# Interleaving transposes with output matmuls, a wider accumulating DMA and a reordered start in a kernel that mixes seven taps and applies a gated two-layer map

## The chip, the cores and the metric

The kernel runs on 1 core of one Trainium2 chip. The metric is device microseconds (us) of one execution. Kernels are compared only within the same rounds.

Short names: PE is the engine of the matmuls, ACT that of activations, DVE the vector engine, POOL the GpSimd engine. A "block" is 1024 tokens; there are 32, numbered 0 to 31.

## The reference, cut to what matters

```python
# x: (8, 4096, 192); weight_gen: (8, 4096, 8 heads, 7 taps)
w = exp(weight_gen - max) / sum                      # softmax over the 7 taps
x_pad = concatenate([zeros(6 rows), x])              # a "halo" of 6 rows ahead of each batch
y[b,s,h,g] = sum_k w[b,s,h,k] * x_pad[b, s+k, h, g]  # 7 products, summed
h = y @ w_in                                         # 192 -> 2048
out = (h - tanh(h)) @ w_out                          # 2048 -> 192
```

## The kernel before

For each block POOL computes the seven products of x with the softmax weights, each 1536 elements in each of 128 partitions. From block 3 on, taps 0, 2, 4 lie in `even`, taps 1, 3, 5 in `odd`, tap 6 in `last`, and a DMA that POOL issues adds `odd` to `even`, so that PE has fewer pieces to sum:

```python
# products(n): on POOL, k = 0..6
if k == K - 2 and in_pairs:                          # after tap 5, before tap 6
    nc.gpsimd.dma_start(out=even[...][:, 0:ACC], in_=odd[...][:, 0:ACC],
                        accum_op=mybir.AluOpType.add, max_dma_last_dim=4096)
# ACC leaves out the last 512 columns, so PE sums one piece of odd itself:
groups = [even[:, i] for i in range(NPAIR)] + [last[:]]
prods_of[n] = [groups + ([odd[:, NPAIR - 1]] if c == NC - 1 else []) for c in range(NC)]
```

PE then transposes and sums the pieces in one go, with matmuls against the identity that accumulate in PSUM (the lines "pc" of the profile). 104 of them make a block's `convT`. The first layer (`gemm1`, "ph") makes 16 f tiles of 128 hidden columns; ACT takes the tanh of each (`th`) and DVE subtracts (`gt`). The second layer (`gemm2`, "obank") makes one of 8 output tiles at a time, for the block before. The pools:

```python
xpool  = tc.tile_pool(name="xpool", bufs=2)          # the x of a block
ppool  = tc.tile_pool(name="ppool", bufs=2)          # even, odd, last
psum_h = tc.tile_pool(name="psum_h", bufs=3, ...)    # shared by ph (f tiles) and pc (transposes)
...
for n in range(NTOT):
    load_wg(n + 3); load_x(n + 3)                    # cases of the first and last blocks, softmax: cut
    for p in range(J):                               # 8 steps: 2 f tiles, 1 output tile
        gemm1(n, 2 * p); gemm1(n, 2 * p + 1)
        gemm2((n - 1) * J + p)
        if p == 0: products(n + 2, behind=last_sub[0])   # POOL may start here, not sooner
        if p == 6: conv(n + 1, (0, 1)); conv(n + 1, (2,))   # the transposes
```

The softmax here doesn't subtract the row's maximum and nothing guards it: scores larger than these inputs give would overflow.

## Time and profile before

770.52 us, median of 3 runs (770.43 to 771.18). The page's busy times and instruction queues:

```profile
PE 736.7 (96%) x14784; PEld 583.1 (76%) x14784; DVE 652.9 (85%) x595; ACT 640.8 (83%) x865; POOL 695.2 (90%) x290
...
q0 software_dynamic: 10816, 31.99, 25.8%
q8 instruction: 115, 1.88, 1.0%
```

The first line is busy us, share of the span and instructions. In the queue lines the columns are packets, MB and share of 16 DMA engines; q0 carries the accumulations, q8 the instructions.

| quantity | value | from |
|---|---|---|
| span | 768.7 us | page |
| PE block without a fetch wait ("undisturbed") | 22.63 us | first transposes at 591.31, 613.94, 636.57 |
| POOL period | 22.656 us | accumulations from block 4 (98.46) to block 31 (710.17), 27 periods |
| distance, POOL's last accumulation to PE's transposes of the same block | 16.92 us | 727.09 - 710.17 |
| transposes to the end | 41.64 us | 768.73 - 727.09 |

The distance rests on these two lines of the timeline (columns as explained below):

```profile
710.17 1.20 POOL L201 DMA_DIRECT2D even<-odd  x1 [0.30 <-POOL odd L192]
...
727.09 0.88 PE L233 MATMUL pc<-ident,even 64*128 64x64 bf16 x48
```

A "fetch wait" is a wait of PE that has no releaser in the trace.

Two views are easily misread. POOL at 90% looks less loaded than PE at 96%; but POOL has nothing to do in the last 55 us, and where it works it works back to back. And in the list of waits, "issue" is a wait with no releaser in the trace, not work.

### The profile page before, as it was taken

The page shows a single profiled execution, that of the slowest core. Times are in us where ns is not written, and L with a number is a line of the kernel's source. Part 1 is how long each engine was busy: PE and PEld are TensorE (multiplying, and loading weights), DVE is VectorE, ACT ScalarE, POOL GpSimd, SP SyncE. Part 2 cuts the span into 40 slices and gives each one's busy share as a digit, 9 for nine tenths or more (in the row PEclk, how much of TensorE's full clock was granted, in tenths as well). Part 3 has the DMA queues.
Part 4 walks back from the last instruction along what each step waited for, and adds up shares of the span by engine and source line. Part 5 has one row for each costly group of instructions (what it writes and reads, how often), then busy time and mean ns, then how long its engine had stood idle before and what let it go on. Part 6 is the DMA issues. An engine that isn't in the chain of part 4 may idle for free.

```text
span 768.7 us, 32330 instructions
## 1 busy us (share of the span) xinstructions
PE 736.7 (96%) x14784; PEld 583.1 (76%) x14784; DVE 652.9 (85%) x595; ACT 640.8 (83%) x865; POOL 695.2 (90%) x290
## 2 busy tenths in 40 slices
PE   2799999999999999999999999999999999999997
PEld 2377787777777777788777777777778777787777
DVE  5987888888898888889888888888888988888883
ACT  1777878888888888888888888888888888888883
POOL 5999999999999999999999999999999999999100
PEclk9999999999999999999999999999999999999999
DMA  7823776555677555577655557765556765542412
GB/s 209 184 81 87 182 181 150 118 145 147 169 182 174 131 129 148 150 180 182 164 123 133 150 160 182 180 128 137 143 150 172 182 181 115 125 142 72 98 43 84
DMA packets 25847, 111.37 MB, mean 145 GB/s; under 512 B 4800, under 2 KB 9456, under 8 KB 21624
## 3 DMA queue, kind: packets, MB, share of 16 engines
q1 hardware_dynamic: 14688, 76.95, 29.9%
q0 software_dynamic: 10816, 31.99, 25.8%
q8 instruction: 115, 1.88, 1.0%
q10 hardware_dynamic: 208, 0.39, 0.2%
q14 instruction: 20, 0.16, 0.1%
HBM read 54.49 MB, written 25.17 MB: 104 GB/s over the span
## 4 chain that ended last, share of the span: by engine, by line
PE 93%; DVE 2%; issue 1%; POOL 1%; DMA 1%; ACT 1%; SPq 0%; POOLq 0%
PE ph L257 43%; PE obank L289 43%; PE pc L233 6%; DVE gt L269 2%; PE po L323 1%; DMA x_t<-in_x_dram 1%; POOL even L192 1%; ACT th L267 0%; ACT convT L244 0%; POOL odd L192 0%; DVE zr L151 0%; DVE zsum L145 0%; SPq L117 0%; SPq L93 0%; SPq L121 0%
## 5 line engine op out<-in xcount | busy, mean ns | idle before, releaser
L269 DVE TENSOR_TENSOR gt<-ph,th 128x1024 bf16<-128x1024 f32 x512 | 602.8, 1219 | 93.3 <-ACT th L267 92.7
L267 ACT ACTIVATE th<-ph 128x1024 f32<-128x1024 f32 x512 | 497.2, 1022 | 65.7 <-PE ph L257 64.9
L257 PE MATMUL ph<-convT,w_in 64*128 64x512 bf16 x3072 | 382.1, 378 | 7.5 <-DVE gt L269 5.0
L289 PEld LDWEIGHTS <-gt 64*128 64x128 bf16 x7936 | 345.1, 94 | 53.4 <-issue 2.5
L289 PE MATMUL obank<-w_out,gt 64*128 64x192 bf16 x7936 | 374.6, 243 | 2.9 <-issue 2.1
L192 POOL TENSOR_TENSOR even<-x_t,wsm 128x1536 bf16<-128x1536 f32 x94 | 272.8, 2903 | 3.9 <-DMA x_t<-in_x_dram 1.6
L192 POOL TENSOR_TENSOR odd<-x_t,wsm 128x1536 bf16<-128x1536 f32 x93 | 269.9, 2903 | 0.0
L257 PEld LDWEIGHTS <-w_in 64*128 64x128 bf16 x3072 | 180.1, 94 | 108.4 <-issue 11.8
L192 POOL TENSOR_TENSOR last<-x_t,wsm 128x1536 bf16<-128x1536 f32 x31 | 103.4, 3336 | 0.0
L307 ACT ACTIVATE out_sb<-obank 128x192 f32<-128x192 f32 x248 | 81.9, 330 | 10.5 <-PE obank L289 4.6
L244 ACT ACTIVATE convT<-pc 128x1024 bf16<-128x1024 f32 x64 | 48.9, 808 | 31.6 <-PE pc L233 31.5
L233 PE MATMUL pc<-ident,even 64*128 64x64 bf16 x2304 | 47.9, 192 | 2.9 <-POOL even L192 1.5
L233 PEld LDWEIGHTS <-even 64*128 64x128 bf16 x2304 | 42.7, 96 | 4.1 <-issue 2.2
L201 POOL DMA_DIRECT2D even<-odd x29 | 34.9, 1205 | 9.1 <-POOL odd L192 9.1
L163 POOL TENSOR_TENSOR wsm<-e_t,zr 128x448 f32<-128x448 f32 x30 | 41.7, 1390 | 0.0
L233 PE MATMUL pc<-ident,odd 64*128 64x64 bf16 x448 | 15.5, 198 | 13.1 <-DVE odd L192 12.8
L135 ACT ACTIVATE e_t<-wg_t 128x448 f32<-128x448 f32 x32 | 18.5, 578 | 8.2 <-DMA wg_t<-in_weight_gen_dram 8.2
L233 PE MATMUL pc<-ident,last 64*128 64x64 bf16 x768 | 23.3, 192 | 1.8 <-issue 1.7
L145 DVE TENSOR_REDUCE zsum<-e_t 128x64 f32<-128x448 f32 x32 | 19.5, 609 | 2.9 <-ACT e_t L135 2.9
L233 PEld LDWEIGHTS <-odd 64*128 64x128 bf16 x448 | 11.3, 100 | 13.6 <-DVE odd L192 12.9
L151 DVE RECIPROCAL zr<-zsum 128x64 f32<-128x64 f32 x30 | 16.6, 553 | 3.0
L233 PEld LDWEIGHTS <-last 64*128 64x128 bf16 x768 | 17.0, 96 | 2.2 <-issue 1.8
(20 smaller groups left out, 48.7 us busy)
## 6 DMA issues: line engine op xcount, KB each, us to landing
x_t<-in_x_dram SPq DMA_DIRECT2D x24, 1344.0 KB
even<-odd POOLq DMA_DIRECT2D x29, 1024.0 KB, 8.8
out_dram<-out_sb SPq DMA_DIRECT2D x31, 768.0 KB
x_t<-in_x_dram SPq DMA_DIRECT2D x8, 1176.0 KB
wg_t<-in_weight_gen_dram SPq DMA_DIRECT2D x32, 224.0 KB
x_t<-in_x_dram SPq DMA_DIRECT2D x8, 157.5 KB
w_in<-in_moe_w_in_dram POOLq DMA_DIRECT2D x6, 128.0 KB, 7.5
w_out<-in_moe_w_out_dram POOLq DMA_DIRECT2D x1, 768.0 KB, 10.8
```

The lines of the kernel that those rows point to most:

```text
L135: nc.scalar.activation(out=e_t[:].rearrange("p j h k -> p (j h k)"), in_=wg_t[:].rearrange("p j h k -> p (j h k)"), func=ACT.Exp,)
L145: nc.vector.reduce_sum(out=zsum[:], in_=e_t[:].rearrange("p j h k -> p (j h) k"), axis=AX.X)
L163: return eng.tensor_mul(wsm.rearrange("p j h k -> p (j h) k"), e_t[:].rearrange("p j h k -> p (j h) k"), zr.rearrange("p (n o) -> p n o", ...
L192: eng.tensor_mul(dst[k].rearrange("p c j h g -> p j h c g"), x_t[:, k : k + J, :].rearrange("p j (h c g) -> p j h c g", h=H, c=NC), w[:, : ...
L201: nc.gpsimd.dma_start(out=even[:].rearrange("p i c j h g -> p (i c j h g)")[:, 0:ACC], in_=odd[:].rearrange("p i c j h g -> p (i c j h g)" ...
L233: nc.tensor.matmul(pc[:, r, col : col + R], lhsT=prods[c][gi][r * R : (r + 1) * R, c, 2 * j : 2 * j + 2].rearrange("p j h g -> p (j h g)") ...
L244: nc.scalar.activation(out=convT[:, c0 : c0 + nch, :].rearrange("p c (j r t) -> p r (c j) t", r=2, t=R), in_=pc[:, :, 0 : nch * JH * R].re ...
L257: nc.tensor.matmul(ph[:, r, :], lhsT=w_in[r * R : (r + 1) * R, c, f * P : (f + 1) * P], rhs=convT[r * R : (r + 1) * R, c, :], start=(c == ...
L267: last_act[0] = nc.scalar.activation(out=th[:], in_=ph_f, func=ACT.Tanh)
L269: last_sub[0] = nc.vector.tensor_sub(gt[:], ph_f, th[:])
L289: mm = nc.tensor.matmul(po[:, 0:D], lhsT=g_of[n][f][r * R : (r + 1) * R, col : col + P], rhs=w_out[r * R : (r + 1) * R, f, :], start=(r == ...
L307: last_act[0] = nc.scalar.activation(out=out_sb[:, j, :], in_=po[:, 0:D], func=ACT.Copy)
```

## The change

The intent: alternate 50 of the transposes with output matmuls, so that PE does not run through its instructions in a burst; put four f-tile steps of the next output tile (the filler) behind the transposes, where PE waits for a PSUM buffer; let the DMA add all of the pairs, so that the last 8 transposes go; load the first x tile ahead of its halo rows, so that POOL starts sooner. The core of the diff (the helper functions it needs are cut):

```diff
-    ACC = NPAIR * J * D - J * R
...
+        if n == 0:
+            rows(0, P, HALO, HALO + J)
+            rows(16, P, 0, HALO)
+            rows(1, 16, 0, HALO)
+            no_halo()
...
-                    out=even[:].rearrange("p i c j h g -> p (i c j h g)")[:, 0:ACC],
-                    in_=odd[:].rearrange("p i c j h g -> p (i c j h g)")[:, 0:ACC],
+                    out=even[:].rearrange("p i c j h g -> p i (c j h g)"),
+                    in_=odd[:].rearrange("p i c j h g -> p i (c j h g)"),
...
-            groups = [even[:, i] for i in range(NPAIR)] + [last[:]]
-            prods_of[n] = [
-                groups + ([odd[:, NPAIR - 1]] if c == NC - 1 else []) for c in range(NC)
-            ]
+            prods_of[n] = [[even[:, i] for i in range(NPAIR)] + [last[:]]] * NC
...
+    LEAD, MIX, FILL = 6, 5, 4
...
-    FA = 8 * P
+    FA = 7 * P
...
-        on_vector=(3, 4, 5, 6),
-        sums=(3, 0, 4, 5, 1, 6, 2),
+        on_vector=(6, 3, 4, 5),
+        order_of=(6, 0, 3, 1, 4, 5, 2),
+        sums=(6, 3, 0, 4, 5, 1, 2),
...
+            if 1 <= n < NTOT - 1 and p == 6:
+
+                pcs = []
+                sums = conv_sums(n + 1, ((0, 1),), pcs)
+                gemm2(
+                    (n - 1) * J + 6,
+                    between=lambda f: [next(sums, None) for _ in range(0 if f < LEAD else MIX)],
+                )
+                for _ in sums:
+                    pass
+                conv_out(n + 1, ((0, 1),), pcs)
+                conv(n + 1, (2,))
+
+                gemm2((n - 1) * J + 7, 0, FILL)
...
+            if 1 <= n < NTOT - 1 and p == 7:
+                gemm2((n - 1) * J + 7, FILL, NFT)
```

## The prediction

> **What bounds the kernel now.** I read the page's chain that ended last, then that chain in order of time around one conv step, then the timelines of PE and POOL, then the DMA view.
>
> ```profile
> PE 93%; DVE 2%; issue 1%; POOL 1%; DMA 1%; ACT 1%; SPq 0%; POOLq 0%
> ...
> 614.12 1.52 PE pc L233 x104
> 615.64 0.02 issue
> 615.65 1.47 PE ph L257 x12
> 617.12 1.32 PE obank L289 x32
> 618.44 1.30 PE ph L257 x12
> ```
>
> The chain is PE for 93% of the span. The second group (start, length, what) is the end of one token block. 32 output matmuls take 1.32 us, 82.5 ns a pair (the two row halves run side by side). 12 matmuls of a pair of f tiles take 1.295 us. 104 transposes take 1.52 us, 14.6 ns each. The first f pair after the transposes takes 1.47 us, not 1.295: about 0.18 us are lost there. The transposes start at 591.49, 614.12 and 636.75, so a block has 22.63 us = 8 x (1.295 + 1.32) + 1.52 + 0.18. So PE has almost no idle time, but not everywhere:
>
> ```profile
> 68.20 0.90 PE L289 MATMUL obank<-w_out,gt 64*128 64x192 bf16 x17 [1.33 <-issue]
> 93.11 0.91 PE L289 MATMUL obank<-w_out,gt 64*128 64x192 bf16 x17 [0.80 <-issue]
> 114.82 0.26 PE L233 MATMUL pc<-ident,last 64*128 64x64 bf16 x6 [1.65 <-issue]
> 502.72 1.25 PE L257 MATMUL ph<-convT,w_in 64*128 64x512 bf16 x10 [0.76 <-issue]
> ```
>
> These waits have no releaser in the trace. Between 45 and 752 us the list of waits has 8 of them on PE, 2.8 + 2.1 + 0.8 = 5.7 us, and each lies within a burst of transposes or just behind one.
>
> Now POOL, one whole period (the next starts at 556.44):
>
> ```profile
> 533.80 2.90 POOL L192 TENSOR_TENSOR even<-x_t,wsm 128x1536 bf16<-128x1536 f32 x1
> 536.66 2.90 POOL L192 TENSOR_TENSOR odd<-x_t,wsm 128x1536 bf16<-128x1536 f32 x1
> ...
> 551.30 1.20 POOL L201 DMA_DIRECT2D even<-odd  x1 [0.30 <-POOL odd L192]
> 552.08 3.37 POOL L192 TENSOR_TENSOR last<-x_t,wsm 128x1536 bf16<-128x1536 f32 x1
> 554.95 1.42 POOL L163 TENSOR_TENSOR wsm<-e_t,zr 128x448 f32<-128x448 f32 x1
> ```
>
> Start to start a product is 2.86 us, the scaling 1.50, and the accumulating DMA costs 0.30 of waiting plus 0.78 until the next product starts. 7 x 2.86 + 1.50 + 1.08 = 22.60; the next period starts 22.64 after this one. POOL is never held up by another engine from 10 us to 714 us. **So POOL's period equals PE's.** This second bound is the main point of the case. The page's chain hides it, because POOL runs ahead: the accumulation for the last block is issued at 710.17 and lands 10.4 us later (8.8 in the median), at about 720, while PE wants it only at 727.27. PE can come forward by some 7 to 8 us before POOL stops it.
>
> **What the Trainium skill says.** "TensorE: Matmul & The Clock Gate", Back-to-back issue gap, gives N/2.4 + 2.5 ns: 82.5 ns for 192 columns and 29.2 ns for 64. The trace agrees: 1.32 us / 16 and 1.52 us / 52. "Advanced Engine Details and Errata", ISA Cache, gives 16 KB cache lines of 256 instructions; the page's queue 8 has 115 instruction packets in 1.88 MB, which is 16 KB each. In a burst PE eats 208 instructions (with the weight loads) in 1.52 us, 137 per us, against 88 in 2.62 us, 34 per us, outside. A fetch that is quick enough elsewhere may be late in a burst: this is my reading of the waits without releaser, and it is inference. "DMA: Bandwidth & Descriptors", SDMA does more than copy, limits an inline add to 2048 elements; the trace has 256 packets of 4 KB (2048 bf16) in each accumulating DMA, two per partition. The same page, in its table of where the fixed 2 us goes, says that many descriptors can be emitted before their cost shows. The trace agrees roughly: the w_out load (2048 rows of 192) holds POOL 1.24 us, each w_in load (64 rows) some 0.56.
>
> **The change, part by part.**
> 1. **Fewer transposes.** The DMA now adds all three pairs of products (it left out the last 512 columns), so the extra 8 transposes of chunk 2 go: 104 becomes 96. 29 blocks x 8 x 14.6 ns = 3.4 us off PE.
> 2. **Filler after the transposes.** DVE's subtraction of the f tile before them ended at 592.97 in the block of 591.31, and the next f pair started at 593.02: that is the 0.18 us, a buffer wait (two of three PSUM buffers go to the transposes). Four f tiles of the next output block, 4 x 82.5 = 0.33 us, now lie there. 1.32 + 96 x 14.6 ns + 0.33 = 3.05 us from the start of the output matmuls, where DVE ends after 2.98. The gap closes: 29 x 0.18 = 5.2 us off PE.
> 3. **Alternation.** 50 of the first 64 transposes go five at a time behind the f tiles 6 to 15. In this stretch 7 matmuls (14 instructions) take 155 ns, so 90 per us: the burst is softened, not gone (46 remain in a row). I take most of the 5.7 us of issue waits as gone, say 4. On the other side, five is odd, so the row halves change places with each f tile; a half slot of 15 ns at each of 10 f tiles costs at most 0.15 us per block, 4 us in all. I take 2.
> 4. **Start.** POOL's first product starts at 10.32 us because x lands then; POOL itself was free at 8.76, after the w_in issues. The first x load was issued behind three small ones and its issue ended near 3.25 us; now it goes right behind the first weights, some 1.3 us sooner, with its halo next. I give POOL 1.1 us. DVE starts with tap 6, which needs no halo, so DVE moves too. The smaller first part of w_in helps the copy that PE waits for at 20.85.
> 5. **Cost of the larger DMA.** 1152 instead of 1024 KB, and since the two sides are laid out as 3 x 1536 elements, 384 packets of 3 KB rather than 256 of 4 KB. Transfer: 6.0 us of each engine now (54.8% of an 11 us window for this queue); by bytes 6.8. I put 0.8 us on the landing, paid once. Issue on POOL: from w_in to w_out, 0.68 us more for 1984 more rows is 0.34 ns each; from w_in to the accumulation, 0.22 us for 192 more is 1.1 ns. For 128 more: 0.04 to 0.15 us, I take 0.08. It is paid by the engine that never rests: 29 x 0.08 = 2.3 us.
>
> **Two sums.** PE alone: 3.4 + 5.2 + 4 - 2 + 1 = 11.6 us, span 768.7 - 11.6 = 757.1. POOL alone: the last accumulation is issued at 710.17 - 1.1 + 2.3 = 711.4 and lands 9.6 us later, at 721.0. From the first transpose to the end it was 768.7 - 727.27 = 41.4 us; with the rest of the output block now behind that first transpose (10 x 155 ns + 46 x 14.6 ns + 0.33 + 1.295 + 12 x 82.5 ns = 4.84 us, against 1.52 + 0.18 + 1.295 + 1.32 = 4.32) it is 41.9. Span 762.9. The later end wins: POOL. The measured time lies 1.8 us above the span (770.5 against 768.7): 764.7.
>
> **Rivals.**
> - **PE stays the bound.** Then 757.1 + 1.8 = 759, or 757 if alternation costs nothing. It needs POOL to gain more than I give it, by a quicker issue or a much earlier start. The back-to-back POOL timeline speaks against it.
> - **The issue of the larger DMA costs POOL much more**, 0.2 to 0.3 us for a three-part pattern instead of one run: 6 to 9 us over 29 blocks, 768 to 771 us, and the change is worth nothing. The 1.24 us of w_out with 2048 rows speaks against it.
> - **Alternation harms PE**: short and long matmuls in turn might uncover weight loads. 0.3 us per block would be hidden behind POOL; only from about 0.5 us does it show, towards 770.
>
> **Range and chances.** The bounds are 757 and 771; most of the weight lies on POOL's chain, whose uncertain parts are the start (0.5 to 2 us) and the issue (1 to 4.5 us). I take 764.5 us, range 759 to 769. Two per cent is 15.4 us: 755.1 would need all of PE's gains and no stop by POOL (4%). Slower by 2% would need a new stall in each block (1%).
>
> **What would show it.** Right: POOL idle nowhere, its period at 22.7 us; a new wait of PE's transposes on the accumulating DMA or on POOL, around 0.3 us per block from about the tenth block on; 96 transposes per block; the 1.47 us f pair back to 1.295; nearly no issue waits. Wrong: transposes that wait for nothing and POOL with idle time (PE bound, 757 to 759), a gap of POOL's DMA row to the next product well above 0.78 us (768 and more), or issue waits of the same sum in another place.

## The result

The changed kernel takes 773.48 us (773.37 to 773.52, 4 runs); the kernel before took 770.57 us (770.43 to 771.18, 4 runs) beside it. The ratio is 1.0036, interval 1.0019 to 1.0053: 0.4% slower and above the predicted range. A ratio here and below is the mean time of one kernel's runs over that of the other's of the same rounds, so it isn't quite the ratio of the medians.

The page after, the same parts as before, with the chain's shares added:

```profile
PE 734.8 (95%) x14552; PEld 574.8 (75%) x14552; DVE 651.2 (84%) x595; ACT 637.3 (83%) x865; POOL 697.7 (90%) x290
...
q0 software_dynamic: 14528, 35.79, 29.1%
q8 instruction: 114, 1.87, 1.0%
...
PE 78%; ACT 9%; DVE 8%; issue 4%; POOL 1%; DMA 0%; POOLq 0%
```

PE has 232 instructions fewer, which is 29 blocks x 8 transposes. q0 has 3712 packets more, 29 x 128. The chain, which was PE for 93%, now passes through ACT and DVE, and "issue" grew from 1% to 4%. This is the end of one block in the chain's order of time (start, length, what):

```profile
594.44 0.43 ACT convT L250
594.88 0.43 issue
595.30 0.59 ACT convT L250
595.90 0.96 ACT th L280
596.86 0.02 issue
596.88 1.24 DVE gt L281
598.12 0.04 issue
598.16 0.82 PE ph L269 x6
```

Behind the transposes the first f tile's way through ACT and DVE is now what PE waits for. One block earlier, the timeline shows the same place (start, length, engine, line, output and inputs, count, and in brackets the idle time and its releaser):

```profile
572.05 0.51 PE L302 MATMUL obank<-w_out,gt 64*128 64x192 bf16 x8
...
572.38 1.47 PE L269 MATMUL ph<-convT,w_in 64*128 64x512 bf16 x12
...
573.25 1.94 ACT L280 ACTIVATE th<-ph 128x1024 f32<-128x1024 f32 x2
573.68 1.17 PE L302 MATMUL obank<-w_out,gt 64*128 64x192 bf16 x24
574.30 2.35 DVE L281 TENSOR_TENSOR gt<-ph,th 128x1024 bf16<-128x1024 f32 x2 [0.81 <-ACT th L280]
574.67 1.52 PE L269 MATMUL ph<-convT,w_in 64*128 64x512 bf16 x10
```

The filler (8 matmuls) stands in front of the first f pair, and the wait there is gone. But within the next f pair, the one of 574.67, a wait of 0.246 us has come in every block: its second tile needs the PSUM buffer that the subtraction from 574.30 on frees. (DVE did not start that sooner because ACT copies `convT` until it starts the tanh at 573.25.) A block without a fetch wait now takes 22.58 us, where it took 22.63.

The waits of PE without a releaser, from the list of waits (us in total, times, longest), the kernel before first:

```profile
PE pc L233 <- issue: 2.8, 5, 1.7
PE obank L289 <- issue: 2.1, 2, 1.3
PE ph L257 <- issue: 0.8, 1, 0.8
```

```profile
PE pc L236 <- issue: 8.6, 8, 2.9
...
PE obank L302 <- issue: 0.5, 1, 0.5
```

They grew from 5.7 to 9.1 us. The list leaves out small gaps. From the starts of the single matmuls, counting each gap of over 45 ns above the usual spacing from 45 us to the end, I get about 7.0 us before and 12.0 us after.

Now POOL in the changed kernel. First two accumulations in the middle of the run (blocks 23 and 24), then the last one (block 31) and PE's first transposes of that block:

```profile
530.79 1.28 POOL L205 DMA_DIRECT2D even<-odd  x1 [0.30 <-POOL odd L196]
...
553.51 1.29 POOL L205 DMA_DIRECT2D even<-odd  x1 [0.30 <-POOL odd L196]
```

```profile
712.60 1.28 POOL L205 DMA_DIRECT2D even<-odd  x1 [0.30 <-POOL odd L196]
...
728.94 0.25 PE L236 MATMUL pc<-ident,even 64*128 64x64 bf16 x5
```

The first two are 22.72 us apart. POOL's period is 22.739 us on average (98.64 to 712.60 in 27 periods), where it was 22.656. POOL never waits for another engine in this stretch. And PE's last transposes follow POOL's last accumulation by 16.34 us, where it was 16.92 before. So the span is made up as follows:

| term, us | before | after | difference |
|---|---|---|---|
| POOL's first accumulation (block 3) | 75.77 | 74.26 | -1.51 |
| to its accumulation of block 4 | 22.69 | 24.38 | +1.69 |
| 27 more periods of POOL | 611.71 | 613.96 | +2.25 |
| distance to PE's transposes, block 31 | 16.92 | 16.34 | -0.58 |
| from there to the end | 41.64 | 42.33 | +0.69 |
| span | 768.73 | 771.27 | +2.54 |

That sum holds by construction. Whether it says anything about cause, that is whether PE is really held at some 16 us behind POOL, is what the experiments had to find out, for PE could by the trace have used a block's accumulation 9.7 us after its issue.

### The profile page after: what moved, and what is told of

The parts are those of the page before. It is cut to its first block, busy times and chain, and to the rows that moved or that the text cites. A ratio compares the mean times of both kernels' runs of the same rounds, so it can differ in the third digit from the quotient of the medians.

```text
span 771.3 us, 31864 instructions
## 1 busy us (share of the span) xinstructions
PE 734.8 (95%) x14552; PEld 574.8 (75%) x14552; DVE 651.2 (84%) x595; ACT 637.3 (83%) x865; POOL 697.7 (90%) x290
## 3 DMA queue, kind: packets, MB, share of 16 engines
q1 hardware_dynamic: 14830, 77.00, 29.7%
q8 instruction: 114, 1.87, 1.0%
## 4 chain that ended last, share of the span: by engine, by line
PE 78%; ACT 9%; DVE 8%; issue 4%; POOL 1%; DMA 0%; POOLq 0%
PE obank L302 37%; PE ph L269 35%; DVE gt L281 7%; ACT th L280 4%; PE pc L236 4%; ACT convT L250 3%; PE po L337 1%; ACT out_sb L321 1%; POOL even L196 1%; DMA wg_t<-in_weight_gen_dram 0%; DVE zsum L149 0%; POOL w_in L372 0%; DVE zr L155 0%; ACT e_t L139 0%; DVE obank L167 0%
## 5 line engine op out<-in xcount | busy, mean ns | idle before, releaser
L302 PE MATMUL obank<-w_out,gt 64*128 64x192 bf16 x7936 | 399.4, 243 | 1.3 <-issue 0.5
L269 PE MATMUL ph<-convT,w_in 64*128 64x512 bf16 x3072 | 386.8, 378 | 8.4 <-DVE gt L281 4.9
L302 PEld LDWEIGHTS <-gt 64*128 64x128 bf16 x7936 | 352.5, 94 | 51.6 <-ACT th L280 0.8
L269 PEld LDWEIGHTS <-w_in 64*128 64x128 bf16 x3072 | 176.4, 94 | 115.5 <-issue 21.9
L236 PE MATMUL pc<-ident,even 64*128 64x64 bf16 x2304 | 69.9, 191 | 7.7 <-issue 3.4
L236 PEld LDWEIGHTS <-even 64*128 64x128 bf16 x2304 | 64.6, 96 | 9.5 <-issue 6.2
L205 POOL DMA_DIRECT2D even<-odd x29 | 37.4, 1289 | 9.0 <-POOL odd L196 9.0
L236 PEld LDWEIGHTS <-last 64*128 64x128 bf16 x768 | 17.3, 96 | 10.9 <-DVE last L196 8.3
L155 DVE RECIPROCAL zr<-zsum 128x64 f32<-128x64 f32 x30 | 16.6, 553 | 3.0
L236 PE MATMUL pc<-ident,odd 64*128 64x64 bf16 x216 | 7.1, 206 | 4.5 <-issue 2.9
L337 PE MATMUL po<-w_out,gt 64*128 64x192 bf16 x256 | 11.0, 243 | 0.0
```

What stands on the lines that cost most here:

```text
L205: nc.gpsimd.dma_start(out=even[:].rearrange("p i c j h g -> p i (c j h g)"), in_=odd[:].rearrange("p i c j h g -> p i (c j h g)"), accum_o ...
L236: nc.tensor.matmul(pc[:, r, col : col + R], lhsT=prods[c][gi][r * R : (r + 1) * R, c, 2 * j : 2 * j + 2].rearrange("p j h g -> p (j h g)") ...
L269: nc.tensor.matmul(ph[:, r, :], lhsT=w_in[r * R : (r + 1) * R, c, f * P : (f + 1) * P], rhs=convT[r * R : (r + 1) * R, c, :], start=(c == ...
L302: mm = nc.tensor.matmul(po[:, 0:D], lhsT=g_of[n][f][r * R : (r + 1) * R, col : col + P], rhs=w_out[r * R : (r + 1) * R, f, :], start=(r == ...
L337: nc.tensor.matmul(po[:, r, 0:D], lhsT=g_of[n][f][r * R : (r + 1) * R, col : col + P], rhs=w_out[r * R : (r + 1) * R, f, :], start=(f == 0 ...
```

## The experiments

Eighteen kernels ran, all with three timed rounds, all correct but one.

### First set: the parts of the change

**e1_nofill**: the change without the filler.

```diff
-                gemm2((n - 1) * J + 7, 0, FILL)
...
-                gemm2((n - 1) * J + 7, FILL, NFT)
+                gemm2((n - 1) * J + 7, 0, NFT)
```

> The changed kernel without its filler: the output block behind the transposes runs whole after the next f pair. Theory 1 (a loop through three PSUM buffers and the tanh and subtraction sets the pace here; the filler only moves the wait from the first f tile behind the transposes to the second f tile of the next block): the 0.246 us gap at that second f tile goes, a gap of about 0.3 us at the first f tile behind the transposes comes (wait for the subtraction), the undisturbed block stays within 0.1 us of 22.58 us, time 773 to 776 us. Rival (the filler does take 0.18 to 0.3 us off each block, the loss is only in the waits without releaser): the block grows to about 22.85 us, time 779 or more.

Measured: 774.04 us against 771.0, ratio 1.0039 (1.0023 to 1.0056). The 0.246 us wait at the second f tile goes, and a wait of 0.294 us in front of the first f pair comes; the block is 22.63 us. The filler only moves the wait: its worth is 0.294 - 0.246 = 0.05 us a block.

**e2_burst**: the change without alternation, all transposes in one burst again (LEAD = 16 instead of 6).

> The changed kernel with all transposes in one burst behind the output matmuls (no alternation), all else kept. Theory 1: PE's own time is not what sets the block, so the undisturbed block stays 22.58 us. Theory 2 (waits without releaser are late instruction fetches at boundaries of 256 PE instructions, and the 896 instructions of a block, 3.5 times 256, bring the boundary to the same place every second block): the waits stay in every second block with about the same sum or more, 10 to 16 us after 45 us; time 772 to 778. Rival (alternation itself stalls PE): the sum of these waits falls to that of the kernel before, 7 us, and the time to about 768.

Measured: 774.07 us, ratio 1.0038 (1.0021 to 1.0056); undisturbed block 22.58 as with alternation. Waits without a releaser are in every second block in both. Alternation neither helped nor harmed.

**s3_start**: the kernel before with the change's start alone (x loads, `order_of`, FA).

> The kernel before with the change's start alone (order of the first loads, tap order of the first products, 7 instead of 8 f tiles in the first part of w_in). If the start is carried to the end: 1.35 us earlier at the second conv step and a time of about 769.4. Rival (swallowed later by fetch waits, since an earlier PE stands differently to the DMA traffic): 770.5 or more.

Measured: 769.46 us against 770.23, ratio 0.9986 (0.9971 to 1.0001). POOL's last accumulation comes at 708.65 instead of 710.17 us. By the ratio the start is worth about 1.1 us and reaches the end; the interval just touches 1, so the size is weakly shown.

**s4_acc**: the kernel before with the accumulation over all pairs alone.

```diff
-                    out=even[:].rearrange("p i c j h g -> p (i c j h g)")[:, 0:ACC],
-                    in_=odd[:].rearrange("p i c j h g -> p (i c j h g)")[:, 0:ACC],
+                    out=even[:].rearrange("p i c j h g -> p i (c j h g)"),
+                    in_=odd[:].rearrange("p i c j h g -> p i (c j h g)"),
```

> The kernel before with the accumulating DMA over all pairs alone (96 transposes for 104; no alternation, no filler, old start). Theory 1: the undisturbed block stays 22.63 us, as the wait for the subtraction behind the transposes grows by the 0.117 us that the eight transposes took. Theory 2: 896 instructions in a block bring the fetch boundary to the same place every second block, and the waits come in every second block; time 771 to 775. Rival (removed transposes come off the time): 767.5.

Measured: 775.38 us, ratio 1.0064 (1.0049 to 1.0079). The undisturbed block stays 22.63: the wait in front of the f pair grows from 0.177 to 0.294 us, by 0.117, which is just the 8 x 14.6 ns of the transposes that went. So fewer transposes bring nothing, and this part alone costs more than the whole change loses. Its page shows the wait that makes the first period longer, which was not foreseen (columns as above):

```profile
POOL odd L191 <- DMA even<-odd: 1.5, 1, 1.5
```

### Second set: what the waits without a releaser are

In the queue lines a q8 packet is 1.87 MB / 114 = 16 KB. PE's 14552 matmuls and as many weight loads over 114 packets make 255 for each, and the last packet need not be full; I take 256. If PE waits for such a packet, its waits must sit at every 256th instruction.

**e3_pad64**: the change with 64 tiny matmuls (128 PE instructions with their weight loads, half a packet) ahead of the first transposes of the run.

```diff
+    pad = psum_h.tile([P, 2, HT], FP32, name="pad", tag="ph")
+    for _ in range(64):
+        nc.tensor.matmul(pad[:, 0, 0:R], lhsT=ident[0:R, :], rhs=ident[0:R, 0:R], start=True, stop=True)
     conv(0, (0, 1), (2,))
```

> The changed kernel with 64 tiny matmuls (128 PE instructions with their weight loads) before the first transposes, where PE is idle. Theory 2 (fetch boundaries): half of 256 instructions moves the boundary by half a line, so the waits without releaser after 150 us move from the blocks with transposes near 160, 207, 253, 344, 435, 526, 617 us to those between them (184, 230, 276 and so on), with a similar sum; time within 3 us of the changed kernel. Rival (they come from the place in the program, or from DMA traffic that repeats with the blocks): the waits stay in the same blocks.

Measured: 774.68 us, ratio 1.0039 (1.0019 to 1.0059). A block of the change has 896 PE instructions, three and a half packets, so a boundary meets the transposes in every second block; half a packet more must move it to the other blocks. The timeline of PE in the changed kernel, then with the padding:

```profile
435.23 0.24 PE L236 MATMUL pc<-ident,last 64*128 64x64 bf16 x5 [0.23 <-issue]
526.33 0.27 PE L236 MATMUL pc<-ident,last 64*128 64x64 bf16 x7 [0.34 <-issue]
617.59 0.30 PE L236 MATMUL pc<-ident,last 64*128 64x64 bf16 x9 [0.79 <-issue]
```

```profile
460.43 0.26 PE L236 MATMUL pc<-ident,last 64*128 64x64 bf16 x5 [0.33 <-issue]
551.55 0.29 PE L236 MATMUL pc<-ident,last 64*128 64x64 bf16 x7 [0.38 <-issue]
```

The same places within the transposes (5, then 7 left of the 16), one block later. The waits are late instruction packets. (Counted through all of PE's instructions in the changed kernel's trace, the eleven waits from 114 to 618 us lie whole multiples of 256 apart.)

**e5_pad32**: the same with 32 tiny matmuls, a quarter of a packet.

> The changed kernel with 32 tiny matmuls (64 PE instructions, a quarter of a fetch line) once at the start, so that the 256-instruction boundaries fall a quarter line later in every block than in the change, as e3_pad64 shifted them by a half. Theory A (late fetches sit at the boundaries, and how late depends on where in the block they fall): the places of the waits within the block shift by 64 instructions, the undisturbed block stays 22.58 us, and the sum of the waits changes (it could be 5 to 15 us): 768 to 775. Rival (the waits are bound to the transposes): they stay at the first transposes, and the time stays at 773.5 to 774.5.

Measured: 773.24 us, ratio 1.0033 (1.0018 to 1.0048); block 22.58. The wait near 526 us moves 32 matmuls forward in its block:

```profile
526.00 0.19 PE L236 MATMUL pc<-ident,even 64*128 64x64 bf16 x1
526.45 0.23 PE L236 MATMUL pc<-ident,even 64*128 64x64 bf16 x4 [0.25 <-issue]
```

(26 transposes and 6 output matmuls lie between this place and that of 526.33 above, which is 64 instructions.) The place follows the packets; the time hardly does: ratios 1.0033, 1.0036 and 1.0039 with the boundary shifted by a quarter of a packet, by none and by a half.

**w1_acc_dummy**: s4_acc with 8 dummy transposes into unused PSUM columns in each block, so that a block has the 912 instructions of before with the larger DMA.

```diff
+        if n not in PLAIN and NC - 1 in parts[-1]:
+            for q in range(JH):
+                for r in range(2):
+                    nc.tensor.matmul(pcs[-1][:, r, HT - R : HT], lhsT=..., rhs=ident[...], start=True, stop=True)
...
```

> The kernel before with the accumulation over all pairs (as s4_acc), and eight dummy transposes into columns of PSUM that nobody reads, behind the last transposes of each block; so the DMA is the larger one and a block has again 912 PE instructions. Theory A (the 896 instructions, three and a half fetch lines, bring the late fetches): the waits called issue after 150 us fall back from about 5 to 6 us to about 2.7, the block is 22.63 us, the time 770.5 to 771.5. Theory B (the larger DMA makes the fetches late): the waits stay at 5 us or more, time 774 to 776 as s4_acc (775.4).

Measured: 775.01 us, ratio 1.0061 (1.0041 to 1.0081), like s4_acc. So theory A fell: it isn't the 896 instructions. It is the larger DMA, or what the larger DMA does to POOL. The block is 22.63 us and POOL's period 22.741.

When is a packet late? One case of the changed kernel, from the trace's DMA records (not a view of the profile):

```
us              on the DMA engines
607.1 - 614.2   x load of a later block, 127 rows of 10,752 bytes
612.3 - 616.0   output store, 128 rows of 6,144 bytes
614.2 - 617.1   load of softmax weights, 128 rows of 1,792 bytes
615.21 - 616.27 instruction packet for PE, 16 KB
617.59          PE goes on with its transposes, after the 0.79 us shown above
```

PE uses a packet's instructions no sooner than 1.2 us after the packet's end; in the eleven late cases it was 1.2 to 1.5 us. Other packets also started near the end of a run of other rows, though PE had no wait from these: at 407.97, the x load's rows having run to 407.9; at 425.99, the accumulation's to 426.0; at 472.51, the accumulation's to 471.8. From 150 to 705 us each packet's transfer started between 0.7 us before and 4.8 us after PE began the packet ahead of it, 1.8 us after in the mean. So packets are fetched one ahead, with a start that varies by over 5 us, and the late starts go together with busy queues. What triggers a fetch isn't in the records, and I leave the rule open.

**s1_split** and **s2_bsplit**: loads of x (from the fourth block on) and output stores cut into eight DMAs of 16 partitions each, in the changed kernel and in the kernel before, so that packets of instructions would find gaps between them.

```diff
+        def chunks(n, p0, p1):
+            step = p1 - p0 if n < 3 else 16
+            for q in range(p0, p1, step):
+                rows(q, q + step)
...
-            rows(0, P)
+            chunks(n, 0, P)
...
+                for q in range(0, P, 16):
+                    nc.sync.dma_start(out=o_v[q : q + 16], in_=out_sb[q : q + 16])
```

> The changed kernel with each load of x from the fourth block on, and each store of the output, cut into DMAs of 16 partitions (one row for each of the 16 engines) instead of 112 or 128; the bytes are the same. Theory 2b (the late instruction fetches are late because they wait behind such a run of 8 rows on their DMA engine: in the changed kernel's trace fetches start when a load or a store ends): the fetches' start after PE enters the line before falls from up to 4.5 us to below 2, and the waits without releaser after 150 us fall from 6.1 us to below 2; undisturbed block still 22.58 us; time about 769. Rival (fetches are late for another reason, or only because of the accumulating DMA, which is not cut): waits and time within 1 us of the changed kernel.

> The same cut of loads and stores in the kernel before. Theory 2b: its waits without releaser after 150 us fall from 2.7 us to below 1; undisturbed block still 22.63 us; time about 769. Rival: unchanged, 770.5 to 771.

Measured: 801.92 us, ratio 1.0404 (1.038 to 1.0429), and 803.2 us, ratio 1.0425 (1.039 to 1.0461). Both expectations missed. Cut this way, each row of x took 1.04 us of a DMA engine instead of 0.57, a load lasted 9.2 to 10.9 us instead of 4.9 to 7.6 (first row's start to last row's end, 150 to 650 us), and this is what PE made of it in s1_split (q1 carries the loads and stores):

```profile
q1 hardware_dynamic: 21438, 77.02, 50.1%
```

```profile
PE pc L241 <- issue: 28.7, 16, 5.8
```

The same bytes took 50.1% of the engines instead of 29.7%, and the late packets cost 28.7 us at this line instead of 8.6. From PE's beginning of a packet to the start of the next one's transfer it took up to 6.3 us, 2.6 in the mean, where it had been 4.8 and 1.8. It is no cure, but a dose: busier DMA engines, later packets.

### Third set: PE made quicker or slower by itself

If late packets were simply a cost of so much per block, PE's own work would add to them or be taken off. **e4_half** makes PE's block shorter: f tiles 13 and 14 have only half of their columns put through tanh and subtraction, so that the PSUM buffer of the transposes comes free sooner. The result is wrong (relative error 0.254).

```diff
+        w = HT if f in (13, 14) else TOK
-        last_act[0] = nc.scalar.activation(out=th[:], in_=ph_f, func=ACT.Tanh)
-        last_sub[0] = nc.vector.tensor_sub(gt[:], ph_f, th[:])
+        last_act[0] = nc.scalar.activation(out=th[:, 0:w], in_=ph_f[:, 0:w], func=ACT.Tanh)
+        last_sub[0] = nc.vector.tensor_sub(gt[:, 0:w], ph_f[:, 0:w], th[:, 0:w])
+        if w < TOK:
+            nc.vector.memset(gt[:, w:TOK], 0.0)
```

> Wrong result on purpose: for f tiles 13 and 14 only half of the columns go through tanh and subtraction, the other half of the output is set to zero. Theory 1: both waits of PE for the subtraction around the transposes vanish, the 0.246 us gap at the second f tile of the next block goes, the undisturbed block falls to 22.33 us (8 x 2.615 + 96 x 14.6 ns), time lower by about 27 x 0.25 = 6.6 us, near 767. Rival (the gap is PE's own, or the drain of one kind of matmul into another): block and time unchanged.

Measured: 771.98 us, ratio 1.0011 (0.9996 to 1.0026). The undisturbed block fell to 22.32 us as expected, so the loop through the PSUM buffers is what sets it. But the time did not follow: in every second block packets came late, and most of these blocks took 22.8 to 23.7 us. PE's list of waits from 115 to 752 us, the changed kernel first, e4_half second:

```profile
PE pc L236 <- issue: 3.7, 6, 1.4
PE pc L236 <- DVE gt L281: 0.8, 1, 0.8
```

```profile
PE pc L236 <- issue: 9.7, 10, 2.1
```

**v1_after_x3** is the change with three x buffers instead of two, meant to take x loads out of the fetches' way; **v4_after_x3_half** is v1 with the tanh and the subtraction of f tiles 12 and 14 each in two halves (a right result, and in the event a slower one), and **v3_start_x3_half** the same on the kernel before with the change's start.

```diff
-    xpool = ctx.enter_context(tc.tile_pool(name="xpool", bufs=2))
+    xpool = ctx.enter_context(tc.tile_pool(name="xpool", bufs=3))
```

```diff
-        last_act[0] = nc.scalar.activation(out=th[:], in_=ph_f, func=ACT.Tanh)
-        last_sub[0] = nc.vector.tensor_sub(gt[:], ph_f, th[:])
+        pieces = (slice(0, HT), slice(HT, TOK)) if f in (12, 14) else (slice(0, TOK),)
+        for w in pieces:
+            last_act[0] = nc.scalar.activation(out=th[:, w], in_=ph_f[:, w], func=ACT.Tanh)
+        for w in pieces:
+            last_sub[0] = nc.vector.tensor_sub(gt[:, w], ph_f[:, w], th[:, w])
```

> The changed kernel with three x buffers instead of two, so a load of x no longer waits until POOL has finished a block's products, and the store of the output queued behind it doesn't either: both should run earlier in PE's block and be over before the transposes. Theory 2b (a late fetch is one that waits behind loads, stores or the accumulation): with that traffic moved away from the transposes the waits without releaser after 150 us fall from 6.1 us to below 2, time 768 to 769.5; undisturbed block 22.58 us. Rival (the traffic has no part, the waits are only a matter of instruction density at the boundary): waits and time as in the changed kernel, 773.

> The changed kernel with three x buffers and the same halves. Theory 1 and 2b together: undisturbed block 22.33 to 22.45 us, few waits without releaser; then POOL with its 22.73 us a block takes over as I had forecast, with transposes that wait for the accumulating DMA or for POOL, and the time is 764 to 767. Rival: 768 or more.

> The same, and tanh and subtraction of f tiles 12 and 14 in two halves each, so that the subtraction can begin after half of the tanh (correct result). Theory 1: the wait behind the transposes, 0.177 us a block, shrinks or goes; undisturbed block 22.46 to 22.55 us, time 763 to 766. Rival (the two further instructions on ACT and DVE cost as much as the earlier begin gains): 22.63 us or more, 767 or more.

Measured: v1 775.48 us, ratio 1.0069 (1.0052 to 1.0085); v4 776.99 us, 1.0089 (1.0073 to 1.0106); v3 773.86 us, 1.0044 (1.0029 to 1.0059). None is an improvement: the halves cost more instructions and the block grew to 22.81 us, and the third x buffer let early x loads get in front of the load of w_out, for which PE then waited. But together with e4 they show something else. In v4, from 115 us on, the list of waits has no "issue" left at all:

```profile
PE ph L269 <- DVE gt L284: 5.9, 28, 0.2
PE pc L236 <- DMA even<-odd: 1.5, 3, 0.7
```

21 of its blocks in a row take 22.81 or 22.82 us. This slower PE has no late packets; the quicker one of e4_half has more. Here are the 27 blocks from the transposes of block 4 to those of block 31 (us):

| kernel | PE's undisturbed block | 27 of these | measured | more than that | POOL's 27 periods | distance at block 31 |
|---|---|---|---|---|---|---|
| e4_half | 22.32 | 602.6 | 616.1 | 13.5 | 614.0 | 15.0 |
| after | 22.58 | 609.7 | 618.2 | 8.5 | 614.0 | 16.3 |
| v1_after_x3 | 22.58 | 609.7 | 618.7 | 9.0 | 613.9 | 14.4 |
| e1_nofill | 22.63 | 611.0 | 616.6 | 5.6 | 613.9 | 16.6 |
| w1_acc_dummy | 22.63 | 611.0 | 618.1 | 7.1 | 614.0 | 16.8 |
| s4_acc | 22.63 | 611.0 | 618.6 | 7.6 | 613.9 | 17.1 |
| v4_after_x3_half | 22.81 | 615.9 | 616.8 | 1.0 | 614.0 | 17.0 |
| before | 22.63 | 611.0 | 615.0 | 4.0 | 611.7 | 16.9 |
| s3_start | 22.63 | 611.0 | 614.4 | 3.4 | 611.7 | 16.3 |

In the rows with the larger DMA, PE's own work spans 13.3 us (602.6 to 615.9) and the measured stretch 2.6 (616.1 to 618.7). Each row is one profiled run, and three kernels that aren't in the table, with the change's DMA and its block of 22.58 us, measured 615.8 (e5_pad32), 618.1 (e2_burst) and 619.0 us (e3_pad64): the stretch varies by 3.2 us with no change in PE's work. So e4 against the change, one edit, says this: of 7.1 us less work for PE 2.1 came in the stretch, and about 1.9 in time (ratios 1.0011 and 1.0036). Most of what PE saves comes back as late packets.

v4 against v1 is one edit too, with 6.2 us more work and a stretch 1.9 us shorter; but PE entered the stretch 9.6 us behind POOL's accumulation in v1 and 14.2 us behind in v4, and by the whole time v4 is 1.5 us slower. In v4 PE's block (22.81 us) is longer than POOL's period (22.74), and the stretch is PE's own 27 blocks and 1.0 us: there PE sets the pace. The same edit with the smaller DMA, v3 against v2, took the stretch from 612.4 to 617.1 us. Where PE's block is the shorter, the stretch goes with POOL's 27 periods, some 2 to 5 us more, by which PE falls back in the first blocks to its distance.

How late the packets are does depend on that distance. In the eleven kernels with two x buffers (without s1, s2 and z1), I compare each block from block 4 on with the undisturbed one, by how far PE stood behind POOL's accumulation at its start:

| distance at the block's start, us | blocks | longer than undisturbed, mean us |
|---|---|---|
| under 15 | 23 | 1.60 |
| 15 to 16 | 55 | 0.37 |
| 16 to 17 | 144 | 0.12 |
| over 17 | 75 | 0.08 |

The 23 all lie in blocks 4 to 9, so an early block could have been another reason; but v2_start_x3 below, which stood at 17.2 us there, lost nothing in its blocks 3 to 8.

### Fourth set: where the DMAs lie

**v2_start_x3**: the kernel before with the change's start and three x buffers. **w2_best**: the same, with the x load of block 3 held back behind the products of block 1, so that w_out comes first.

> The kernel before with the change's start and three x buffers. Theory 2b: waits without releaser after 150 us fall from 2.8 us to below 1, time near 767; undisturbed block 22.63 us. Rival: 769.5, as with the start alone.

> The kernel before with the change's start alone and three x buffers, the x load of block 3 held back until the products of block 1 are issued so that it does not delay the load of w_out. v2_start_x3 lost about 6 us at the start to that delay, and ran 22.72 us a block from the third convolution on. Theory (late fetches are tied to x loads that wait for their buffer): the start is as in s3_start (third convolution at about 61.5 us), 29 blocks of 22.72 us make 658.9, and the end is 42 us: span 762.5, time about 764.5 (763 to 767). Rival (the third buffer only moves the DMAs to other fetches): as s3_start, 769.5, or worse.

Measured: v2 770.88 us, ratio 1.0006 (0.9991 to 1.0021); w2 769.56 us, 0.999 (0.9975 to 1.0005). In v2 PE waited once for w_out:

```profile
PE obank L294 <- DMA w_out<-in_moe_w_out_dram: 3.2, 1, 3.2
```

and the granted clock was 0.5 for the 6.8 us that followed. w2 removed that wait, but a late packet of 2.5 us took its place, and 22.78 us a block on average instead of the hoped-for 22.72 did the rest. The expectation of 764.5 missed; both are no better than s3_start.

**w4_fill1**: the change with the old accumulation, no alternation, one filler tile and w2's x buffers. One tile splits the wait of 0.177 us between two places (some 0.11 and 0.01 us were left).

```diff
-    LEAD, MIX, FILL = 6, 5, 4
+    LEAD, MIX, FILL = 16, 5, 1
```

> The changed kernel with the old, smaller accumulation (104 transposes instead of 96), no alternation, one filler tile of the next block instead of four, and three x buffers with the delayed load as in w2_best. One filler tile splits the wait for the PSUM buffer between two places. Theory: undisturbed block 22.5 to 22.6 us, waits as in w2_best: 762 to 764.5. Rival (the filler only moves the wait, as e1_nofill showed for four tiles, and late fetches differ at random): as w2_best or up to 3 us slower.

Measured: 768.54 us (766.47 to 769.49) against 770.39, ratio 0.9969 (0.9947 to 0.999). This is the quickest of all, 0.3% under the kernel before; but the 762 to 764.5 us expected missed too. Block 22.56 us, POOL 22.657 us a period, distance 16.29 us at the end.

**z1_late_acc**: the change with the accumulation issued behind the last product, to make POOL quicker by the 0.30 us that it waits in front of that DMA.

```diff
-            if k == K - 2 and in_pairs:
+            if k == (K - 2 if n == 2 else K - 1) and in_pairs:
```

> The changed kernel with one edit: from the fourth block on, POOL issues the accumulating DMA behind the last product instead of ahead of it. POOL then no longer waits 0.30 us for the product that the DMA reads; its period falls from 22.738 to about 22.43 us and lies below PE's undisturbed 22.58. The same bytes move, 2.6 us later in POOL's period. Theory A (POOL paces PE at a distance): with POOL quicker, the late fetches have nothing to hold PE back to; from about 150 us on they shrink from 6.1 us to under 2. PE at its own pace: first transposes of the fourth block at 87.8 plus 28 x 22.58 = 720.0, plus 42.3 = 762.3. If the distance of 16.3 us between accumulation and transposes stays as well: the second accumulation at 101.2 plus 27 x 22.43 plus 16.3 plus 42.3 = 765.4. So span 762 to 766, time 764 to 768. Theory B (late fetches depend on the load of the DMA queues only): waits and time stay, 772 to 775.

Measured: 804.9 us, ratio 1.0456 (1.043 to 1.0483). Neither theory had this. The last product frees the x tile, so the x load of a later block now starts ahead of the accumulation, and the accumulation lands later. The page's line of DMA issues (KB, median us from issue to landing), the changed kernel first, z1 second:

```profile
even<-odd POOLq DMA_DIRECT2D x29, 1152.0 KB, 9.7
```

```profile
even<-odd POOLq DMA_DIRECT2D x29, 1152.0 KB, 16.5
```

Now PE does wait for it, and POOL waits for PE at the head of its next block (the two lists of waits of z1):

```profile
PE pc L236 <- DMA even<-odd: 25.2, 14, 9.7
```

```profile
POOL wsm L167 <- DVE gt L281: 31.4, 26, 3.7
```

So z1 did not test POOL's speed, as it was meant to. It shows what a direct wait for the accumulation looks like, and that the distance of 16 us is no such wait in the change: there the list has none.

### Last: POOL made slower by itself

**z3_pool_slow**: the kernel before, with one small clear of a spare tile on POOL in each block, which nobody reads.

```diff
+    spare = const.tile([P, 256], FP32, name="spare")
...
+        if n not in PLAIN:
+            nc.gpsimd.memset(spare[:], 0.0)
```

> The kernel before with one more operation on POOL in each block from the third on: clearing a spare tile of 256 words per partition that nobody reads (estimated 0.2 to 0.5 us, from 0.2 us for the 128 half words of the identity). Call its cost d, read from POOL's period, 22.656 us now. PE's undisturbed block stays 22.63 us. Theory A (PE cannot come nearer to POOL than some 16 us, because its late fetches hold it there): the distance of PE's transposes to POOL's accumulation ends at 16 to 17.5 us, the late waits grow by nearly as much as POOL loses, and the time is 770.6 plus about 28 d, thus 779 for d = 0.3. Theory B (POOL's pace matters only where PE waits for it directly): PE goes at its own pace, the distance shrinks by d a block from 16 us to about 8 or 9 us, the late waits stay at about 7 us, and the time is 770 to 772.

Measured: 772.57 us (772.49 to 772.68) against 770.31, ratio 1.0029 (1.0012 to 1.0046). The clear is there in each period:

```profile
511.69 1.43 POOL L164 TENSOR_TENSOR wsm<-e_t,zr 128x448 f32<-128x448 f32 x1
512.60 0.77 POOL L180 MEMSET spare<- 128x256 f32 x1
513.20 3.03 POOL L195 TENSOR_TENSOR even<-x_t,wsm 128x1536 bf16<-128x1536 f32 x1
```

POOL's period became 22.756 us, so d is 0.10 us, less than I had estimated, since the clear mostly overlaps the operation ahead of it. Theory A then asks for 770.3 + 28 x 0.10 = 773.1, theory B for the time of before. 2.3 of the 2.8 us came, and PE's undisturbed block stayed 22.63. The late packets of blocks 4 to 31 grew from 4.0 to 5.9 us. The last distance is 15.8, a little under A's 16. This leans to A, at a small dose; at this size it isn't proof by itself.

## Why the prediction was wrong

Its main idea, that POOL and not PE sets the end, fits the runs, though not by the direct wait for the accumulation that it had forecast. Its sum for POOL was a span of 762.9 us; measured were 771.27. The 8.4 us lie in three terms:

| term of the POOL sum | predicted | measured | off by |
|---|---|---|---|
| last accumulation issued | 711.4 | 712.60 | +1.2 |
| from there to the transposes | 9.6 | 16.34 | +6.7 |
| from there to the end | 41.9 | 42.33 | +0.4 |

**The step that failed** is "PE can come forward by some 7 to 8 us before POOL stops it". The prediction let PE come up to the landing of the accumulation. In the runs with two x buffers in which PE never waited for the accumulation itself, it did not come nearer than 15.0 us in the last twenty blocks: PE's instruction packets came late, and the more so the nearer PE stood to POOL (1.60 us a block under 15 us, 0.12 at 16 to 17). That a quicker PE does not come through is shown by e4_half. v4_after_x3_half shows that the late packets go when PE's block is longer than POOL's period; there PE's own block sets the pace. That POOL's pace carries the end is supported by z3_pool_slow, and by w1_acc_dummy and s4_acc, which change the DMA too. No fixed limit is shown: e4_half (15.0) and e5_pad32 (15.7) were still coming nearer at the end. Why the distance is about 16 us is argued only: the runs of accumulation, x load and store that keep the DMA engines busy are timed by POOL (its accumulation, and the x tile that its last product frees), a packet that PE wants in such a run starts late, and a PE that comes forward against POOL meets them. That three x buffers changed the distance to 14.4 us (v1) and 17.6 (w2) fits, as they move the x loads; no run has isolated it, and in v1 the accumulation landed 13.4 us after its issue (median) and PE waited for it directly, 2.5 us in three blocks.

By its own steps:

1. **Fewer transposes**, 3.4 us off PE: wrong. The instructions went, but PE waits behind them for a PSUM buffer that comes free at a time of its own; s4_acc's wait grew by the same 0.117 us a block. The gain of this step hung on the cure of step 2.
2. **Filler**, 5.2 us off PE: wrong. It moved the wait by one f tile (0.246 us a block, e1_nofill). The prediction asked what would fill the gap and not what the gap's buffer chain (f tile, tanh, subtraction, buffer) would do next. Steps 1 and 2 together left 0.05 us a block, 1.4 us in all.
3. **Alternation**, 4 of 5.7 us of issue waits gone, 2 lost: wrong in its premise. The waits are late packets, as it had inferred, but a lower rate of instructions did not avoid them; e2_burst without alternation has the same time. The profile's sum rose to 9.1 us, near what its last paragraph had named as a sign of error ("issue waits of the same sum in another place").
4. **Start**, 1.1 us: right mechanism; POOL gained 1.51 us at block 3, and s3_start alone gains about 1.1 us in time, by a ratio whose interval reaches 1.0001.
5. **Cost of the larger DMA**: 0.08 us a block on POOL predicted, 22.739 - 22.656 = 0.083 measured; landing 0.8 later predicted, 9.7 - 8.8 = 0.9 measured. Both right. Not foreseen: POOL's one wait of 1.6 us for its own accumulation, which eats the gain of the start.

Of the rivals, the second named the right place, the larger DMA on POOL, with the wrong size; alternation was harmless. Of what was to show the prediction right, POOL's 22.7 us, no idle POOL (but for the one wait of 1.6 us) and 96 transposes came; so did the f pair behind the transposes at 1.295 us, by the starts of its matmuls, but the pair after it took 0.25 us more. The direct wait of the transposes for the accumulation and the vanishing of issue waits did not come.

So the change's balance is this: the start gives POOL 1.5 us; the wider accumulation takes 1.7 us once and 2.25 us over 27 periods; everything done for PE is worth 0.05 us a block and comes back as late packets; PE's end part is 0.7 us longer.

## What to carry to other kernels

When two engines have the same period, saving on one brings nothing until the other is quicker: add up each engine's chain by itself, with its start and its tail, and do not assume that the slack between them can be used in full; look for how near they have ever come. If work next to a buffer wait is removed or added, follow that buffer's chain one turn further, for the wait often just moves. And before waits without a releaser are put down to a local cause, make the engine slower on purpose: if they vanish, as in v4_after_x3_half, they were not a fixed cost but slack against something else.

## What the Trainium skill lacked or had wrong

- "Advanced Engine Details and Errata", ISA Cache: the line of 256 instructions agrees (e3_pad64 and e5_pad32 move the waits by exactly half and a quarter of 256). Neither it nor another page that I found says that a fetch is held up by other transfers: here 5.7 us of waits before and 9.1 after, 32.8 us (28.7 and 4.1) with busier DMA engines (s1_split), and 1.2 to 1.5 us from a packet's end to its use.
- "Perfetto Trace Analysis", DMA Optimizations, says that splitting DMAs into smaller sections may complete sooner if the engines are generally idle. With queues that took some 60% of the engines here, eight DMAs of 16 partitions instead of one of 128 made a row take 1.04 us instead of 0.57 and the kernel 4% slower. The page gives no figure for such a split.
- No page that I found says how long two large transfers that overlap delay each other: the accumulation landed 16.5 us after its issue, instead of 9.7, when it was issued behind the x load (z1_late_acc).
